# Two gated linear-attention branches: the low-weight terms of the last, half-filled chunk of K, Q and V moved into 64-row matmuls

## The chip, the cores and the metric

The kernel runs on one core of a Trainium2 chip, in float32 data (float32r operands for the large matmuls). The metric is the device time of one launch in microseconds (us); the smaller, the better. Engines are named as in the profile: PE (matmul), PEld (weight load into PE), DVE, ACT, POOL and SP (which issues the DMAs).

## The reference

Two branches A and B share x (2048 tokens, 448 features, 16 heads of 28) and are mixed by a gate:

```python
def branch(x, wqkv, w_phi, wo):                    # B=1, S=2048, D=448, H=16, Dh=28
    q, k, v = split_heads(x @ wqkv)
    pq, pk = q @ w_phi, k @ w_phi                  # per head, 28 x 28
    phi_q = concat(softmax(pq), softmax(-pq))      # 56 features
    phi_k = concat(softmax(pk), softmax(-pk))
    kv, z = phi_k.T @ v, phi_k.sum(over s)         # sums over all tokens
    return ((phi_q @ kv) / (phi_q @ z + 1e-6)) @ wo

g = sigmoid((x * gate_w).sum(-1))
out = g * branch(x, *A) + (1 - g) * branch(x, *B)
```

## The kernel before, in words

**Tiling.** The 2048 tokens are 16 tiles of 128. `xt`, the transposed x, and the weights come in chunks of 128 feature rows: 448 rows are three full chunks and one of 64 rows. The rows of the last chunk are there twice, so chunk 3 fills all 128 partitions. Every float32 operand is split into a high part (rounded to float32r) and a low part. For x, `split_x` (L306) makes chunks 0 to 3 of the high part, writes the low part of chunk 3 into the upper 64 partitions of chunk 3 itself, and puts the low parts of chunks 0 to 2 into chunks 4 to 6 (`xs`, seven chunks of 256 tokens for one pair of tiles, three such buffers).

**K, Q and V.** For a tile and a branch b, `mms` (L416) runs eleven matmuls into one PSUM bank, by the list `XT` (L414): (chunk of x, high or low weights, chunk of the weights).

```python
    XT = [(c, 0, c) for c in range(4)] + [(c, 1, c) for c in range(4)] + [(4 + c, 0, c) for c in range(3)]
```

Term (3, 0, 3) multiplies the high and the low half of x's last chunk with the high weights; term (3, 1, 3) multiplies both halves with the low weights, of which only the lower 64 partitions (high x times low weights) carry what is needed. `k_proj` (L471), `q_proj` (L511) and `v_proj` (L457) call `mms` for b = 0 and 1: banks `K0` and `K1`, the two banks of `Q`, and `VA` and `VB`. The projections for K and Q already contain `w_phi`, which `fold` put into the weights at the start.

**What follows a projection.** `v_out` (L463): ACT copies VA and VB into `vs`, and for branch A takes the gate's exponential into `glog`. `k_soft` (L475): ACT copies K0 and K1 into `pk`; then come two reductions on DVE, two subtractions on POOL, two exponentials on ACT, two sums on DVE and two multiplications on POOL, into one of three buffers `es`. `q_front` (L515): DVE reduces Q over the feature axis, subtracts, and SP sends the result through DRAM (`qd`) for a turn of the layout. `q_soft` (L532, steps "S") loads it back, makes both softmaxes (ACT, DVE, POOL) and transposes on DVE; for tiles 0 to 7 the result goes to DRAM (`spill`) until it is fetched back. `kv_acc` (L496, steps "kv") adds two tiles' states phi_k.T @ v into bank `T0` with small matmuls, `T<-ret,vs`, of 29 columns by 56.

**After the last tile.** The states are turned (`kv_turn`), and for every two tiles come 32 x 32 matmuls into four banks `N` (`num`, L581), a DVE transpose, a reciprocal, mixing by the gate on POOL, more transposes, and 21 matmuls per tile with the output weights into `O0` or `O1` (`out_mm`, L631).

**The order.** `steps` (L109) writes the order of the work out by hand. PE follows it strictly. On the other engines `Plan.order` (L53) sorts: each step has a cost and a due time worked out backwards along its dependencies, and a free engine takes the ready step that is due first. The instructions of an engine then run in that fixed order, each waiting for its inputs. In the loop over p in 2..6 of `steps` one iteration treats K of tiles 2p and 2p+1, Q of tiles 2p-2 and 2p-1, V of tiles 2p+2 and 2p+3, and one kv step in its middle, behind the first Q.

Of the kernel before, what the change touches and what calls it, by code (L numbers as in the profile page):

```python
# [13 lines left out]
P = 128  # L14
# [94 lines left out]
def steps():  # L109
# [4 lines left out]
    yield from (("S", 0, JIT % 3 - 1), ("K", 2), ("Q", 1), ("S", 1, (JIT - 1) % 3 - 1), ("k", 3, 0), ("k", 3, 1), ("vm", 5, 0), ("kv", 0, 1), ("vo", 5, 0), ("ks", 3), ("V", 5, 1))  # L114
    for p in range(2, 7):
        yield "x", p + 1
        yield "K", 2 * p
        yield "Q", 2 * p - 2
        if 2 * p - 2 < JIT:
            yield "S", 2 * p - 2, (JIT - 2 * p + 2) % 3 - 1  # L120
        yield "kv", 2 * p - 2, 2 * p - 1
        yield "wo", p - 2
        if p == 3:
            yield "wo", 6
        if p < 6:
            yield "V", 2 * p + 2
        yield "K", 2 * p + 1
        yield "Q", 2 * p - 1
        if 2 * p - 1 < JIT:
            yield "S", 2 * p - 1, (JIT - 2 * p + 1) % 3 - 1  # L130
        if p < 6:
            yield "V", 2 * p + 3
        if p == 6:
            yield "gates", 0, 12
            yield "gates_b", 0, 12
    yield from (("K", 14), ("V", 14, 0), ("k", 15, 0), ("k", 15, 1), ("kv", 12, 13), ("wo", 5), ("load_wo",), ("Q", 12), ("ks", 15), ("V", 14, 1), ("V", 15, 0), ("q", 13, 0), ("q", 13, 1))
# [30 lines left out]
def hedgehog_mix(ctx: ExitStack, tc: tile.TileContext, xd, wv, wkt, wqt, wphi, wo, cmask, cpmask, out):  # L167
# [18 lines left out]
    rq = sb.tile([P, 2, 8 * FW], F32R, name="rq")  # L186
    rx = sb.tile([P, NX, 14 * P], F32R, name="rx")
    ret = sb.tile([P, 3 * 2048 + NE * 4 * D], F32, name="ret")
# [50 lines left out]
    def free_v():  # L239
# [38 lines left out]
    def low_part(eng, n, o, a, h, r, w, **k):  # L278
        put(eng, n, tt(eng, o, a, h, OP.subtract), r, w, two=True, **k)
# [40 lines left out]

# [94 lines left out]

    def mms(t, w, name, k, lo, hi):  # L416
        x, o = xs[t // 2 % NX], t % 2 * P
        def go():
            for i, (xc, l, c) in enumerate(XT):
                nc.tensor.matmul(bank[name][:, k, lo:hi], x[:, xc, o:o + P], w[l][:, c], start=i == 0, stop=i == len(XT) - 1)  # L420
        return go

    def xkeys(t):
        return [("x", t // 2 % NX, t % 2), ("xl", t // 2 % NX, t % 2)]

    def feat(w, b):
        return [x[:, b].rearrange("p c f h -> p c (f h)") for x in w]
# [272 lines left out]
    for what, *a in steps():  # L700
# [125 lines left out]
```

## Time and profile before

| | us |
|---|---|
| median of 3 timed runs | 337.41 (337.08 to 338.82) |
| the profiled execution's own time | 338.86 |
| its span, first to last instruction of the program | 337.0 |
| PE busy / PEld busy | 329.7 / 295.5 |
| DVE busy / POOL busy / ACT busy | 280.6 / 250.8 / 145.2 |

The span is what the trace covers; the profiled execution's own time has 1.86 us more around it. A busy PE means that some matmul was in flight: matmuls overlap, each lasts 0.36 us in the record while a new one starts about every 0.2 us, so the busy share doesn't say how fast PE goes. What it costs is read from the distance between matmuls, and from the chain of work that ended last, which gives every piece the time by which it moved the end.

### The profile page before, as it was taken

What the parts mean: (1) busy time and instruction counts of PE and PEld (TensorE: products, weight loads), DVE (VectorE), ACT (ScalarE), POOL (GpSimd) and SP (SyncE); (2) the same over time, 40 slices, a digit from 0 to 9 for tenths busy, and PEclk for the clock granted to TensorE, in tenths of its full rate; (3) what the DMA queues carried; (4) which work ended last, traced back from release to release, by engine and by line L of the source; (5) the groups of instructions that cost most, each with busy time, mean ns of one, the idle gap of its engine ahead of it and who ended that gap; (6) DMA issues with size and microseconds to landing.
All of it is one profiled execution on the core that took longest, in us unless ns stands there. A gap on an engine that the chain in (4) does not pass through costs nothing.

```text
span 337.0 us, 8897 instructions
## 1 busy us (share of the span) xinstructions
PE 329.7 (98%) x3742; PEld 295.5 (88%) x3742; DVE 280.6 (83%) x339; ACT 145.2 (43%) x236; POOL 250.8 (74%) x210
## 2 busy tenths in 40 slices
PE   7999999999999999999999999999999999999994
PEld 6977899998999999999999999999788888788894
DVE  3648879699797896969899979797899999999960
ACT  3747944372365462624445344432052433523331
POOL 7018669999999969989896999694269768887400
PEclk9999999999999999999999999999999999999999
DMA  7773046531297757647646330765886355131011
GB/s 248 215 244 97 2 125 189 165 119 41 70 336 251 217 187 191 238 136 238 217 123 262 88 110 15 277 255 182 236 255 236 135 191 197 61 147 56 31 54 55
DMA packets 29871, 54.73 MB, mean 162 GB/s; under 512 B 4632, under 2 KB 25480, under 8 KB 27528
## 3 DMA queue, kind: packets, MB, share of 16 engines
q1 hardware_dynamic: 29576, 54.06, 48.7%
q8 instruction: 29, 0.48, 0.6%
q0 software_dynamic: 256, 0.12, 0.1%
q14 instruction: 10, 0.08, 0.1%
HBM read 31.54 MB, written 24.22 MB: 165 GB/s over the span
## 4 chain that ended last, share of the span: by engine, by line
PE 65%; DVE 18%; POOL 8%; DMA 4%; issue 3%; ACT 1%; SPq 1%; DVEq 0%; POOLq 0%; ACTq 0%
PE Q L420 15%; PE K L420 14%; PE O L636 10%; PE VA L420 8%; PE VB L420 8%; POOL ret L263 3%; PE T L505 3%; DVE rv L599 3%; POOL rv L608 3%; DVE ret L551 3%; PE N L588 2%; DMA ret<-in_wv 2%; DVE sm L493 2%; DVE rx L263 1%; DVE qsm L546 1%
## 5 line engine op out<-in xcount | busy, mean ns | idle before, releaser
L420 PE MATMUL Q<-rq,rx 128*128 128x432 f32 x352 | 72.1, 359 | 0.0
L420 PE MATMUL K<-rk,rx 128*128 128x432 f32 x352 | 71.8, 359 | 0.0
L636 PE MATMUL O<-rk,rx 128*128 128x448 f32 x336 | 70.6, 368 | 0.1
L636 PEld LDWEIGHTS O<-rk,rx 128*128 128x128 f32 x336 | 62.5, 188 | 8.5 <-ACT rx L627 1.2
L420 PEld LDWEIGHTS Q<-rq,rx 128*128 128x128 f32 x352 | 65.9, 188 | 3.8 <-DVE ru L263 0.4
L420 PEld LDWEIGHTS K<-rk,rx 128*128 128x128 f32 x352 | 66.1, 188 | 3.1
L266 ACT ACTIVATE ret<-ret 128x896 f32<-128x896 f32 x48 | 45.7, 951 | 46.3 <-POOL ret L263 45.3
L263 POOL TENSOR_TENSOR ret<-ret,sm 128x896 f32<-128x896 f32 x32 | 53.9, 1707 | 2.4 <-DVE sm L494 2.2
L493 DVE TENSOR_REDUCE sm<-ret 128x32 f32<-128x896 f32 x32 | 33.8, 1070 | 6.2 <-ACT ret L266 6.2
L551 DVE STREAM_TRANSPOSE ret<-ret 128x2048 f32<-128x2048 f32 x16 | 36.5, 2283 | 0.9 <-POOL ret L263 0.6
L263 POOL TENSOR_TENSOR ret<-pk,mx 128x896 f32<-128x896 f32 x16 | 27.3, 1707 | 11.6 <-DVE mx L486 11.6
L546 DVE TENSOR_REDUCE qsm<-ret 128x32 f32<-128x896 f32 x32 | 33.3, 1058 | 2.6 <-ACT ret L266 2.5
L420 PE MATMUL VA<-rv,rx 128*128 128x450 f32 x154 | 34.3, 370 | 0.0
L420 PE MATMUL VB<-rv,rx 128*128 128x448 f32 x154 | 33.9, 367 | 0.0
L263 POOL TENSOR_TENSOR ret<-qmn,ru 128x896 f32<-128x896 f32 x16 | 28.2, 1765 | 6.9 <-DVE ret L551 4.2
L266 ACT ACTIVATE ret<-ru 128x896 f32<-128x896 f32 x16 | 15.2, 951 | 42.1 <-issue 19.6
L420 PEld LDWEIGHTS VB<-rv,rx 128*128 128x128 f32 x154 | 28.6, 188 | 3.4 <-issue 0.8
L420 PEld LDWEIGHTS VA<-rv,rx 128*128 128x128 f32 x154 | 28.6, 189 | 2.9 <-ACT rk L266 0.4
L263 POOL TENSOR_TENSOR ret<-ret,qsm 128x896 f32<-128x896 f32 x16 | 27.3, 1705 | 0.9
L263 POOL TENSOR_TENSOR ret<-mx,pk 128x896 f32<-128x896 f32 x16 | 27.3, 1707 | 0.7 <-DVE mx L487 0.7
L540 DVE TENSOR_REDUCE qmn<-ru 128x32 f32<-128x896 f32 x16 | 17.0, 1062 | 10.6 <-DMA ru<-qd 10.5
L608 POOL TENSOR_TENSOR rv<-rv,rd 128x896 f32<-128x896 f32 x14 | 23.8, 1703 | 1.1
(92 smaller groups left out, 443.6 us busy)
## 6 DMA issues: line engine op xcount, KB each, us to landing
ed<-ret SPq DMA_DIRECT2D x8, 1024.0 KB
ret<-ed SPq DMA_DIRECT2D x8, 1024.0 KB
qd<-ru SPq DMA_DIRECT2D x64, 112.0 KB
ru<-qd SPq DMA_DIRECT2D x16, 448.0 KB
out<-ret SPq DMA_DIRECT2D x16, 224.0 KB
wod<-wst SPq DMA_DIRECT2D x14, 224.0 KB
rk<-wod SPq DMA_DIRECT2D x2, 1568.0 KB
xraw<-in_xt SPq DMA_DIRECT2D x5, 512.0 KB
```

The lines of the kernel that those rows point to most:

```text
L263: return lambda: ENG[eng].tensor_tensor(val(o), val(a), val(b), op)
L266: return lambda: A.activation(val(o), val(i), f, **k)
L420: nc.tensor.matmul(bank[name][:, k, lo:hi], x[:, xc, o:o + P], w[l][:, c], start=i == 0, stop=i == len(XT) - 1)
L493: put("DVE", 2 * D, lambda s=s, e3=e3: V.tensor_reduce(sm[:, s], e3, AX.X, OP.add), [ke[s], *([("u", 0, 1)] if t == 15 else [])], [("sm", ...
L505: nc.tensor.matmul(kvp()[32 * r:32 * r + DH + 1, b, g], vs[t % NV][:, b, h // 2, h % 2], es[t % NE][:, :, hs:hs + DH], start=(t == 0 and b ...
L540: put("DVE", 2 * D, lambda: V.tensor_reduce(qmn, tq.rearrange("p c b g f -> p c (b g) f"), AX.X, OP.min), [kt, *late], [kn])
L546: put("DVE", 2 * D, lambda s=s, e3=e3: V.tensor_reduce(qsm[:, s], e3, AX.X, OP.add), [ke[s], *late], [("qsm", i, s)])
L551: add("DVE", 2.25, lambda: V.transpose(eTf[slot], eq.rearrange("p s a c f -> p (s a c f)")), ke, turned(slot))
L588: nc.tensor.matmul(bank["N"][32 * g:32 * g + 32, r, 2 * b * P:2 * b * P + 2 * P], kvt[32 * r:32 * r + 32, b, s, g], eTp[slots[0] // 2][32 ...
L599: add("DVE", 0.07 + 1.08 * nt, lambda: V.transpose(ctr().rearrange("p (r n) -> p r n", r=4), bank["N"][:, :, :2 * nt * P]), ["N"], [("ctr" ...
L608: put(eng, 2 * D, lambda: ENG[eng].tensor_tensor(mid["o", n % 3].rearrange("p (c a f) -> p a c f", c=4, a=8), ctv()[:, :, i, :, :DH], rd[: ...
L636: nc.tensor.matmul(bank[pb][:, 0, :D], a, w, start=i == 0, stop=i == len(terms) - 1)
```

## The change

For the iterations p = 2 to 5 term (3, 1, 3) is left out of the eleven of K and Q (tiles 4 to 11 and 2 to 9) and of V (tiles 6 to 12): steps "k10", "q10" and "v10" run ten terms and leave the PSUM group open. A new step "halves" then closes the open groups of one K tile, one Q tile and (from V tile 6 on) one V tile at once, with two matmuls of 64 rows for each: branch 0 in partitions 0 to 63, branch 1 in partitions 64 to 127. For branch 1 the upper 64 partitions need the high part of x's last chunk, so `xs` gets an eighth chunk, which ACT fills from the upper copy of the raw rows (`xd`). The product of the low x with the low weights, which the full term added as well, is no longer in these tiles' sums.

Since a group stays open until "halves", all banks of K, Q and V close together; the copies and reductions that follow are listed behind "halves", V of the next tile runs right behind them, and V tiles 7, 9, 11, 13 and 15 use bank `O0` in place of `VA`. The kv step stands behind the second "halves" of an iteration rather than in its middle. Iteration p = 6 is written out with full terms. `wp` and `wpd`, which are needed only at the start, now lie in `kvt`, which is needed only at the end.

```diff
-    for p in range(2, 7):
+    for p in range(2, 6):
         yield "x", p + 1
-        yield "K", 2 * p
-        yield "Q", 2 * p - 2
-        if 2 * p - 2 < JIT:
-            yield "S", 2 * p - 2, (JIT - 2 * p + 2) % 3 - 1
-        yield "kv", 2 * p - 2, 2 * p - 1
-        yield "wo", p - 2
...
-        if p < 6:
-            yield "V", 2 * p + 2
-        yield "K", 2 * p + 1
-        yield "Q", 2 * p - 1
...
+        for i in range(2):
+            k, q, v = 2 * p + i, 2 * p - 2 + i, 2 * p + 1 + i
+            yield "k10", k
+            yield "q10", q
+            yield "halves", k, q, v if v >= 6 else None
+            if i:
+                yield "kv", q - 1, q
+            yield "ks", k
+            yield "qf", q
+            if v >= 6:
+                yield "vo", v, 0
+                yield "vo", v, 1
+            yield "S", q, (JIT - q) % 3 - 1
...
+            yield "v10" if k < 11 else "V", v + 1
+    yield from (("x", 7), ("K", 12), ("Q", 10), ("wo", 4), ("k", 13, 0), ("k", 13, 1), ("kv", 10, 11), ("ks", 13), ("Q", 11), ("gates", 0, 12), ("gates_b", 0, 12))
...
-    rx = sb.tile([P, NX, 14 * P], F32R, name="rx")
+    rx = sb.tile([P, NX, 16 * P], F32R, name="rx")
...
-    wp = sb.tile([P, 2, 4, HP], F32, name="wp")
-    wpd = sb.tile([P, 2, 4, HP], F32, name="wpd")
...
+    wp, wpd = kvt[:, 0], kvt[:, 1]
...
+        if p < 7:
+            put("ACT", hi - lo, act(t[64:P, 7, :], r[64:P, 3, :]), [*kr, *l], [("xd", n, i) for i in range(lo // P, hi // P)])
...
-    def mms(t, w, name, k, lo, hi):
+    def mms(t, w, name, k, lo, hi, part=False):
         x, o = xs[t // 2 % NX], t % 2 * P
+        terms = [a for a in XT if not part or a != (3, 1, 3)]
         def go():
-            for i, (xc, l, c) in enumerate(XT):
-                nc.tensor.matmul(bank[name][:, k, lo:hi], x[:, xc, o:o + P], w[l][:, c], start=i == 0, stop=i == len(XT) - 1)
+            for i, (xc, l, c) in enumerate(terms):
+                nc.tensor.matmul(bank[name][:, k, lo:hi], x[:, xc, o:o + P], w[l][:, c], start=i == 0, stop=i == len(terms) - 1 and not part)
         return go
+
+    def halves(k, q, v):
+
+        keys, banks_, go = [], [], []
+        for t, kind in ((v, "v"), (k, "k"), (q, "q")):
+            if t is not None:
+                x, o = xs[t // 2 % NX], t % 2 * P
...
+                    banks_.append(kb)
+                    go.append((name, i, lo, n, x[64 * b:64 * b + 64, 7 if b else 3, o:o + P], w[64 * b:64 * b + 64, 3]))
+        def run():
+            for name, i, lo, n, a, w in go:
+                nc.tensor.matmul(bank[name][:, i, lo:lo + n], a, w, start=False, stop=True)
+        add("PE", 0.3 + 0.1 * len(go), run, keys, list(dict.fromkeys(banks_)))
...
     def v_bank(t, b):
-        return (f"K{b}", 0, ("K", b)) if t == 1 else (("VA", "VB")[b], 0, ("VA", "VB")[b])
+        n = "O0" if b == 0 and t >= 7 and t % 2 else ("VA", "VB")[b]
+        return (f"K{b}", 0, ("K", b)) if t == 1 else (n, 0, n)
```

The first place is PE in the iteration p = 3. K_99, K_100 (K_97, K_98 in the changed kernel) are the banks K0 and K1, O_556 is O0, T_557 is T0. Before:

```order
L420 MATMUL K_99<-rk,rx 128x432 x11
L420 MATMUL K_100<-rk,rx 128x432 x11
L420 MATMUL Q<-rq,rx 128x432 x22
L505 MATMUL T_557<-ret,vs_74 29x56 x32
L505 MATMUL T_557<-ret,vs_70 29x56 x32
L420 MATMUL VA<-rv,rx 128x450 x11
L420 MATMUL VB<-rv,rx 128x448 x11
```

and in the changed kernel, the second half of iteration p = 3:

```order
L422 MATMUL VA<-rv,rx 128x450 x10
L422 MATMUL VB<-rv,rx 128x448 x10
L422 MATMUL K_97<-rk,rx 128x432 x10
L422 MATMUL K_98<-rk,rx 128x432 x10
L422 MATMUL Q<-rq,rx 128x432 x20
L447 MATMUL VA<-rv,rx 128x450
L447 MATMUL VB<-rv,rx 128x448
L447 MATMUL K_97<-rk,rx 128x432
L447 MATMUL K_98<-rk,rx 128x432
L447 MATMUL Q<-rq,rx 128x432 x2
L533 MATMUL T_557<-ret,vs_74 29x56 x32
L533 MATMUL T_557<-ret,vs_70 29x56 x32
```

Each of the six banks has one full matmul less, and six matmuls of 64 rows (L447) stand in a row behind the last full one; the kv step follows them.

The second place is ACT where it empties the banks of V tile 7 and K tile 6; in the changed kernel these close in one "halves", and VB must be empty before V of tile 8 may use it, K0 before K of tile 7. Before:

```order
L266 ACTIVATE ret<-ru 128x32x28
L266 ACTIVATE vs_72<-VB 128x16x28
L266 ACTIVATE wst<-wst 128x448
L266 ACTIVATE ret<-ret 128x32x28
L266 ACTIVATE pk_68<-K_99 128x448
L266 ACTIVATE pk_68<-K_100 128x448
```

and in the changed kernel:

```order
L265 ACTIVATE ret<-ret 128x896 x2
L265 ACTIVATE ret<-ru 128x32x28
L265 ACTIVATE vs_72<-VB 128x16x28
L265 ACTIVATE pk_68<-K_97 128x448
L265 ACTIVATE pk_68<-K_98 128x448
L265 ACTIVATE vs_72<-O_556 128x16x28
L265 ACTIVATE glog<-O_556 128x1
```

The copies out of PSUM now stand side by side, and VB's stands behind exponentials that wait for POOL (`ret<-ret`) and for a DMA (`ret<-ru`).

## Rows read from the trace of the kernel before

**Rows 1.** The page: busy time, and the granted clock in 40 slices of the span.

```profile
PE 329.7 (98%) x3742; PEld 295.5 (88%) x3742; DVE 280.6 (83%) x339; ACT 145.2 (43%) x236; POOL 250.8 (74%) x210
PEclk9999999999999999999999999999999999999999
```

**Rows 2.** Waits of PE: engine, line, who was waited for; total us, times, longest.

```profile
PE VA L452 <- ACT rv L266: 1.1, 1, 1.1
PE VB L645 <- DVE zero L654: 1.1, 1, 1.1
PE T L505 <- POOL ret L263: 0.7, 1, 0.7
```

**Rows 3.** The chain that ended last, 98 to 139 us: start us, us, what.

```profile
98.52 4.32 PE K L420 x22
102.84 4.31 PE Q L420 x22
107.14 1.71 PE T L505 x128
108.85 2.45 PE VA L420 x11
111.31 2.23 PE VB L420 x11
...
122.16 2.26 PE VA L420 x11
...
136.99 2.44 PE VA L420 x11
```

**Rows 4.** The same chain from 231 us on.

```profile
236.48 2.70 PE N L588 x115
239.21 2.33 DVE rv L599
...
292.48 3.52 PE O L636 x16
```

**Rows 5.** Timeline of PE at the kv step of 78 us: start us, us, what.

```profile
78.05 0.99 PE L505 MATMUL T<-ret,vs 128*29 128x56 f32 x64
79.74 0.99 PE L505 MATMUL T<-ret,vs 128*29 128x56 f32 x64 [0.70 <-POOL ret L263]
80.67 0.87 PE L420 MATMUL VA<-rv,rx 128*128 128x450 f32 x3
```

**Rows 6.** Timeline of PE where it changes from full to small matmuls and back.

```profile
106.78 0.36 PE L420 MATMUL Q<-rq,rx 128*128 128x432 f32 x1
107.07 1.78 PE L505 MATMUL T<-ret,vs 128*29 128x56 f32 x128
...
108.78 0.47 PE L420 MATMUL VA<-rv,rx 128*128 128x450 f32 x1
```

**Rows 7.** Timeline of PE and PEld behind a group of N; N's durations (ns, min/median/max).

```profile
257.54 0.46 PE L588 MATMUL N<-ret,kvt 32*32 32x256 f32 x6
257.92 0.48 PE L636 MATMUL O<-rk,rx 128*128 128x448 f32 x1
...
257.92 0.30 PEld L636 LDWEIGHTS O<-rk,rx 128*128 128x128 f32 x2 [0.41 <-issue]
...
L588 PE MATMUL N<-ret,kvt x1024: 373/375/400, 236.4 to 315.1; 32*32 32x256 f32 x171
```

**Rows 8.** Groups of matmuls and loads: count, busy us, mean ns of one.

```profile
L420 PE MATMUL VA<-rv,rx 128*128 128x450 f32 x154 | 34.3, 370 | 0.0
...
L420 PEld LDWEIGHTS K<-rk,rx 128*128 128x128 f32 x352 | 66.1, 188 | 3.1
...
L588 PEld LDWEIGHTS N<-ret,kvt 32*32 32x32 f32 x1024 | 14.4, 103 | 6.2 <-issue 1.8 <-DVE qsm L546 0.3 <-DVE rv L625 0.3
```

**Rows 9.** Three iterations: PE, PEld, DVE, ACT, POOL busy; clock; DMA share; GB/s.

```profile
79.64:107.77 28.13, 28.03 (x252) 26.29 (x256) 23.66 (x28) 12.81 (x21) 27.54 (x22) 1.00 0.59 200
107.77:135.90 28.13, 28.13 (x276) 26.39 (x268) 22.90 (x27) 13.50 (x21) 25.11 (x18) 1.00 0.65 204
135.90:164.02 28.12, 28.12 (x277) 26.36 (x268) 24.23 (x30) 13.04 (x21) 24.86 (x18) 1.00 0.64 217
```

**Rows 10.** ACT: copies out of VB and K, its copies of x, and its waits.

```profile
113.57 0.55 ACT L266 ACTIVATE vs<-VB 128x448 f32<-128x448 f32 x1 [1.62 <-PE VB L420]
...
115.74 0.54 ACT L266 ACTIVATE pk<-K 128x448 f32<-128x448 f32 x1 [0.33 <-PE K L420]
...
L266 ACT ACTIVATE rx<-xraw x8: 402/1042/1062, 4.5 to 180.8; 128x1024 fp32r<-128x1024 f32 x5, 128x512 fp32r<-128x512 f32 x2, 128x256 fp32r<-128x256 f32 x1
...
ACT ret L266 <- POOL ret L263: 45.3, 35, 6.5
```

**Rows 11.** Windows ahead of the last phase and in it, columns as in rows 9.

```profile
220.00:240.00 20.00, 20.00 (x334) 17.67 (x333) 16.70 (x26) 4.07 (x9) 11.14 (x8) 1.00 0.67 228
260.00:280.00 20.00, 20.00 (x305) 16.97 (x304) 19.55 (x21) 7.42 (x12) 14.93 (x15) 1.00 0.50 178
```

More of the change, by code (lines that the diff above doesn't have):

```diff
@@ L114, in steps @@
     yield from (("S", 0, JIT % 3 - 1), ("K", 2), ("Q", 1), ("S", 1, (JIT - 1) % 3 - 1), ("k", 3, 0), ("k", 3, 1), ("vm", 5, 0), ("kv", 0, 1), ("vo", 5, 0), ("ks", 3), ("V", 5, 1))
[L115 removed]
+    for p in range(2, 6):
         yield "x", p + 1
[L117 to L135 removed]
+        for i in range(2):
[11 more added lines that the diff above has]
+            yield "S", q, (JIT - q) % 3 - 1
+            if i == 0:
+                yield "wo", p - 2
+                if p == 3:
+                    yield "wo", 6
+            yield "v10" if k < 11 else "V", v + 1
+    yield from (("x", 7), ("K", 12), ("Q", 10), ("wo", 4), ("k", 13, 0), ("k", 13, 1), ("kv", 10, 11), ("ks", 13), ("Q", 11), ("gates", 0, 12), ("gates_b", 0, 12))
     yield from (("K", 14), ("V", 14, 0), ("k", 15, 0), ("k", 15, 1), ("kv", 12, 13), ("wo", 5), ("load_wo",), ("Q", 12), ("ks", 15), ("V", 14, 1), ("V", 15, 0), ("q", 13, 0), ("q", 13, 1))
@@ L221, in hedgehog_mix @@
     wvh, wvl = (rv[:, i].rearrange("p (c n) -> p c n", c=4) for i in range(2))
-    xs = [rx[:, i].rearrange("p (k t) -> p k t", k=7) for i in range(NX)]
+    xs = [rx[:, i].rearrange("p (k t) -> p k t", k=8) for i in range(NX)]
     es = [re[:, i].rearrange("p (s n) -> p s n", s=2) for i in range(NE)]
@@ L245, in free_v @@
         mid["oT", 0], mid["oT", 1] = f[:, 6784:7168], ref[:, 4992:5376]
-    hls = [rx[:, i].rearrange("p (s k t) -> p s k t", s=2, k=7) for i in range(NX)]
+    hls = [rx[:, i, :14 * P].rearrange("p (s k t) -> p s k t", s=2, k=7) for i in range(NX)]
     obs = [ref[:, 4096 + D * i:4096 + D * i + D] for i in range(2)]
@@ L414, in hedgehog_mix @@
     XT = [(c, 0, c) for c in range(4)] + [(c, 1, c) for c in range(4)] + [(4 + c, 0, c) for c in range(3)]
-    def mms(t, w, name, k, lo, hi):
+    def mms(t, w, name, k, lo, hi, part=False):
         x, o = xs[t // 2 % NX], t % 2 * P
+        terms = [a for a in XT if not part or a != (3, 1, 3)]
         def go():
-            for i, (xc, l, c) in enumerate(XT):
-                nc.tensor.matmul(bank[name][:, k, lo:hi], x[:, xc, o:o + P], w[l][:, c], start=i == 0, stop=i == len(XT) - 1)
-        return go
+            for i, (xc, l, c) in enumerate(terms):
+                nc.tensor.matmul(bank[name][:, k, lo:hi], x[:, xc, o:o + P], w[l][:, c], start=i == 0, stop=i == len(terms) - 1 and not part)
+        return go
+    def halves(k, q, v):
[3 more added lines that the diff above has]
+                x, o = xs[t // 2 % NX], t % 2 * P
+                keys += xkeys(t) + [("xd", t // 2 % NX, t % 2)]
+                for b in range(2):
+                    if kind == "v":
+                        (_, w), n = v_weights(b)
+                        name, i, kb = v_bank(t, b)
+                        lo = 0
+                        keys.append(("vl", 3, b))
+                    else:
+                        w = feat(((wkh, wkl), (wqh, wql))[kind == "q"], b)[1]
+                        name, i, kb = (f"K{b}", 0, ("K", b)) if kind == "k" else ("Q", b, "Q")
+                        lo, n = FO, FZ - FO
+                        keys += wkeys(kind, (b,))
+                    banks_.append(kb)
[4 more added lines that the diff above has]
+        add("PE", 0.3 + 0.1 * len(go), run, keys, list(dict.fromkeys(banks_)))
     def xkeys(t):
@@ L455, in v_first, with v_proj @@
             v_out(t, b)
-    def v_proj(t, b):
+    def v_proj(t, b, part=False):
         w, n = v_weights(b)
         n_, k, kb = v_bank(t, b)
-        add("PE", 11 * 0.203, mms(t, w, n_, k, 0, n),
+        add("PE", (11 - part) * 0.203, mms(t, w, n_, k, 0, n, part),
             xkeys(t) + [("v" + h, c, b) for h in "hl" for c in range(4)], [kb])
@@ L469, in v_out, with k_proj @@
             add("ACT", 0.2, act(glog[:, t:t + 1], lambda: bank[n_][:, k, D:D + 1], AF.Exp, scale=-1.0), [kb], [("gl", t)], ahead=9.0 * (t < 2))
-    def k_proj(t, b):
-        add("PE", 11 * 0.197, mms(t, feat((wkh, wkl), b), f"K{b}", 0, FO, FZ),
+    def k_proj(t, b, part=False):
+        add("PE", (11 - part) * 0.197, mms(t, feat((wkh, wkl), b), f"K{b}", 0, FO, FZ, part),
             xkeys(t) + wkeys("k", (b,)), [("K", b)])
@@ L509, in kv_acc, with q_proj @@
             [k for t in ts for k in (("e", t % NE, 0), ("e", t % NE, 1), ("v", t % NV, 0), ("v", t % NV, 1))], ["T0"])
-    def q_proj(t, b):
-        add("PE", 11 * 0.197, mms(t, feat((wqh, wql), b), "Q", b, FO, FZ),
+    def q_proj(t, b, part=False):
+        add("PE", (11 - part) * 0.197, mms(t, feat((wqh, wql), b), "Q", b, FO, FZ, part),
             xkeys(t) + wkeys("q", (b,)), ["Q"])
@@ L720, in hedgehog_mix @@
             q_front(*a)
+        elif what in ("k10", "q10", "v10"):
+            for b in range(2):
+                {"k": k_proj, "q": q_proj, "v": v_proj}[what[0]](*a, b, True)
+        elif what == "halves":
+            halves(*a)
         elif what == "Q":
```

## The prediction

> **What bounds the kernel now.** I read the page first. PE is busy for 98% of the span and its granted clock reads 9 tenths or more in every slice [rows 1], 1.00 in the middle [rows 9], the upper of its two levels (2.4 GHz), so no slow clock explains the time. But DVE is at 83% and POOL at 74%, so the page alone doesn't settle the bound. PE's waits do: three in all, two of them at the start and one of 0.7 us behind POOL [rows 2]. The chain that ended last then shows from 98 us on nothing but PE, piece behind piece: 22 matmuls of K in 4.32 us, 22 of Q in 4.31, eleven of V in 2.23 or 2.26 [rows 3]. One matmul of 432 columns thus costs 4.32/22 = 0.196 us, one of 448 or 450 about 2.245/11 = 0.204. The distance follows the columns, though a weight load alone lasts 0.188 us in the record [rows 8]. From 239 us on the chain runs over DVE, until it comes back to PE at 292 [rows 4]. So in the stretch that the change touches (about 67 to 180 us) PE is the bound, and a matmul taken out is worth its distance, if nothing else becomes late.
>
> **Terms taken out and put in.** K loses one term in 8 tiles and 2 branches, Q as many: 32 x 0.196 = 6.27 us. V loses it in 7 tiles: 14 x 0.204 = 2.86. Together 9.13 us. In their place come 46 matmuls of 64 rows, in 23 pairs whose two members use different halves of the rows and different banks. No matmul of 64 rows is in this trace. From below a pair costs one slot (0.196 or 0.204), from above two. The nearest rows are those of N, 32 x 32 pieces of 256 columns, whose group has 115 of its matmuls in 2.70 us, 0.023 each [rows 4]. By the distance above, 256 columns one after another would take 256/432 x 0.196 = 0.116 us each; so about five run at a time. I take one slot: 23 pairs cost 16 x 0.196 + 7 x 0.204 = 4.56, and **4.57 us** are saved.
>
> **Changes of shape.** PE goes from full rows to half rows and on in eight places. What such a change costs is in the trace. The last Q starts at 106.78 and the first T at 107.07 [rows 6]: 0.29 in place of 0.196, so 0.095 for letting the array run empty. The first V behind T then lasts 0.47 us, where its kind has a mean of 0.370 [rows 6, 8]: 0.10 for a weight load that nothing covers. The way in costs about 0.095 + 0.10 = 0.20 us, as the half-row load has 128 columns like the full one. For the way out I have two neighbours: behind Q the emptying costs the same 0.095; behind N the last matmul starts at 257.54 + 0.46 - 0.375 = 257.625 and the first O at 257.92, 0.295 in place of 0.116, so 0.18 [rows 7]. Half rows lie between the two shapes, so I take 0.14. In four of the eight places full rows follow (0.14 + 0.10 = 0.24); in the other four T follows, which paid 0.095 for its way in before and now pays 0.14, so 0.045 more, and T's way out is as before. Sum: 8 x 0.20 + 4 x 0.24 + 4 x 0.045 = **2.7 us lost**. The terms net 4.57 - 2.74 = 1.8 us. A middle iteration (two trips of three pairs) should shrink by 0.5, from 28.1 to 27.6 us; the first has one trip of two pairs and shrinks by 0.3.
>
> The Trainium skill says, in TensorEngine Tiling (Array Packing), Key Properties, that a change of tiling mode, not merely of tile, drains TensorE; its Overview promises up to twice the speed for 64 rows. By the second alone the terms would give 4.6 us, with the first 1.8; the trace agrees with the first, by the 0.095 and 0.18 us above.
>
> **The kv step.** At 78 us T's first 64 matmuls start at 78.05, the other 64 wait for POOL until 79.74, and V follows at 80.67 [rows 5]. That is 2.62 us, against 107.07 to 108.78 = 1.71 in the next iteration [rows 6]. In the changed kernel this step stands half an iteration (some 13 us) later, while the multiplications it waits for ended at 79.7. So **0.9 us** go. What would be late next is the split of x for V of tile 6, which PE now reaches at 78; its subtractions on POOL stand ahead of K's there, and no step of K needs POOL sooner than the kv step does. I take nothing for it.
>
> **Edits at nothing.** ACT gets eight copies of 64 partitions: four of 256 columns, at most 0.40 us each by the 256-column form, and four of 128 [rows 10]; under 3 us in all on an engine at 43% [rows 1]. If that cover fails, a copy holds up what stands behind it on ACT (a rival below). `wp` in `kvt`, the larger `rx` and V in `O0` use space that is idle then. POOL's and DVE's work is only reordered; POOL has 27.5, 25.1 and 24.9 us in iterations of 28.1 [rows 9], so it fits into 27.6, barely in the first. SP issues the same DMAs, though the load of x and those of the output weights change places with q's; q's load is needed a whole half-iteration later.
>
> **Does the end follow?** The chain's DVE part begins with the transpose at 239.21, which N's end releases [rows 4], and in the 20 us before, DVE works 16.7 and POOL 11.1 us [rows 11]; neither carries a backlog there, so what PE gains ahead of N arrives at the end.
>
> **Sum.** 1.8 + 0.9 = 2.7 us. The profiled execution goes from 338.86 to 336.2 and its span from 337.0 to 334.3. The median of the timed runs is 1.45 below that execution, so I forecast **334.7** for it. With a drain of 0.095 or 0.18 on every way out and some tenths for small waits, this case reaches from 333.9 to 335.6. About 0.5% (1.7 us, so 335.7 and 339.1) is what a measurement of this kernel can tell from no change.
>
> **The rivals.**
> Loads in series: the two loads of a pair go one after the other. Two full loads behind N start 0.30 - 0.19 = 0.11 us apart [rows 7]; a pair then takes 0.22 in place of 0.198 (23 x 0.022 = 0.5 lost), and each way in shows a second bare load (8 x 0.11 = 0.9). The gain falls to 1.3: 336.1. For it: a load of 32 columns lasts 103 ns and a full one 188 [rows 8], so columns count. Against: N's loads come as often as its matmuls, every 0.023 us. The Trainium skill, TensorE: Matmul & The Clock Gate, LDWEIGHTS, speaks for the first step of this rival: the time of a load follows its columns alone, so half the rows save nothing. 15%.
> No overlap: pairs need two slots. Then only the changes of shape and the kv step remain: 337.4 + 2.74 - 0.9 = **339.3, slower**. It decides where a pair takes over 0.198 + 2.7/23 = 0.32 us, and by over 0.5% near two slots. For it: T's 56 columns would take 0.025 us each alone and take 1.71/128 = 0.013, so only two of its four column pieces overlap. Against: N. 8%.
> ACT is late: VB is read behind "halves" and written again behind ten terms, 0.24 + 2.05 us later, of which the copy takes 0.55 [rows 10]; 1.7 us are left in the three places without T. ACT runs in order, and its exponentials waited for POOL 35 times, at most 6.5 us [rows 10]. If such a wait reaches 1.7 us past "halves", PE stands: 1 us in all of three places gives 337.7, 2 us 340.7. Before, K, Q and VA lay between, 4.32 + 4.31 + 2.26 us [rows 3]. 12%.
> The end doesn't follow: DVE has 19.6 of 20 us in the last phase [rows 11]. If its backlog, not N, set the start, the gain would be lost: 337.4. 8%.
> Cheaper changes: half rows need no drain, and the change does all its terms promise: 337.4 - 4.57 - 0.9 = 331.9. 7%.
>
> **How the numbers follow.** My forecast has 50%. Faster by over 0.5%: 50 + 7, a quarter of loads in series (4) and 2 of the late ACT, 0.63. Slower by over 0.5%: most of no overlap (6) and 5 of the late ACT, 0.11. Within: 0.26. The range takes the forecast, loads in series, the lost end and a late ACT of up to 1 us: 332.6 to 338.0; outside lie the other cases and half of the cheap one.
>
> **What would show it.** Right: in the timeline a first half-row matmul 0.29 us behind the last Q, pairs 0.2 apart, and the next shape 0.3 behind the last pair; V to V in the chain 27.6 us; no wait of T; no wait of PE for ACT. Wrong: pairs 0.3 or more apart, "PE VB <- ACT" or "PE K <- ACT" among the waits, or a last phase that starts earlier and ends no earlier.

## The result, and the profile of the changed kernel

| | before | changed |
|---|---|---|
| median of 20 timed executions | 337.78 us | 339.73 us |
| their range | 336.96 to 340.93 | 336.59 to 341.82 |
| profiled execution: own time, span | 338.86, 337.0 | 340.17, 338.4 |

The ratio is 1.0046, 95% interval [1.0025, 1.0067]: the changed kernel is half a per cent slower, where 0.8% faster was forecast. (Ratios leave out executions that lie over 1.5% above the fastest of their kernel.)

The page's busy times, PE's waits, and three iterations from one end of Q to the next but one (columns as in rows 9):

```profile
PE 329.1 (97%) x3742; PEld 290.4 (86%) x3742; DVE 284.5 (84%) x339; ACT 146.8 (43%) x244; POOL 251.0 (74%) x210
PEclk9999999999999999999999999999999999999999
```
```profile
PE Q L422 <- DVE ru L262: 3.1, 1, 3.1
PE VB L673 <- DVE zero L682: 1.1, 1, 1.1
PE VA L480 <- ACT rv L265: 0.5, 1, 0.5
PE K L422 <- ACT pk L265: 0.3, 1, 0.3
PE Q L422 <- ACT rk L265: 0.3, 1, 0.3
```
```profile
79.06:106.68 27.62, 27.62 (x262) 24.99 (x261) 23.93 (x28) 12.13 (x20) 27.23 (x21) 1.00 0.54 187
106.68:134.31 27.63, 27.63 (x262) 25.02 (x261) 25.14 (x28) 12.70 (x22) 25.28 (x19) 1.00 0.63 212
134.31:161.93 27.62, 27.62 (x262) 25.01 (x261) 24.12 (x29) 13.76 (x23) 25.58 (x19) 1.00 0.64 213
```

The iterations did shrink, from 28.13 [rows 9] to 27.62 us, and PE has no gap in them; T's wait [rows 2] is gone. But PE now stands 3.1 us in front of a Q, which it never did before. Two stretches of PE's timeline show the gain and the loss, half rows first (start us, us, what):

```profile
117.71 0.76 PE L422 MATMUL Q<-rq,rx 128*128 128x432 f32 x3
118.40 0.47 PE L447 MATMUL VA<-rv,rx 64*128 64x450 f32 x1
118.40 0.47 PE L447 MATMUL VB<-rv,rx 64*128 64x448 f32 x1
118.70 0.37 PE L447 MATMUL K<-rk,rx 64*128 64x432 f32 x2
118.89 0.37 PE L447 MATMUL Q<-rq,rx 64*128 64x432 f32 x2
119.20 0.40 PE L533 MATMUL T<-ret,vs 128*29 128x56 f32 x16
...
188.61 0.94 PE L422 MATMUL Q<-rq,rx 128*128 128x432 f32 x4
189.85 0.65 PE L422 MATMUL K<-rk,rx 128*128 128x432 f32 x2 [0.30 <-ACT pk L265]
...
195.60 0.53 PE L533 MATMUL T<-ret,vs 128*29 128x56 f32 x28
199.23 0.66 PE L422 MATMUL Q<-rq,rx 128*128 128x432 f32 x2 [3.10 <-DVE ru L262]
```

The two members of a pair start together (their weight loads at 118.39 and 118.40, 0.18 us each); pairs are 0.30 and 0.19 us apart, and T follows 0.31 behind the last. The Q that ends at 189.55 is tile 10's, the one at 199.23 tile 11's. It waits for the bank that DVE empties with `qmx` (the maximum) and two subtractions into `ru`. DVE's timeline there, of the changed kernel and then of the kernel before:

```profile
187.74 1.09 DVE L521 TENSOR_REDUCE sm<-ret 128x32 f32<-128x896 f32 x1 [2.72 <-ACT ret L265]
...
191.74 1.07 DVE L574 TENSOR_REDUCE qsm<-ret 128x32 f32<-128x896 f32 x1
192.72 1.08 DVE L514 TENSOR_REDUCE mx<-pk 128x32 f32<-128x896 f32 x1
193.72 1.08 DVE L515 TENSOR_REDUCE mx<-pk 128x32 f32<-128x896 f32 x1
194.71 2.30 DVE L579 STREAM_TRANSPOSE ret<-ret 128x2048 f32<-128x2048 f32 x1
196.94 1.05 DVE L548 TENSOR_REDUCE qmx<-Q 128x32 f32<-128x896 f32 x1
198.02 1.16 DVE L262 TENSOR_TENSOR ru<-Q,qmx 128x448 f32<-128x448 f32 x2
```
```profile
185.41 1.07 DVE L493 TENSOR_REDUCE sm<-ret 128x32 f32<-128x896 f32 x1
...
188.33 1.03 DVE L486 TENSOR_REDUCE mx<-pk 128x32 f32<-128x896 f32 x1
189.27 1.07 DVE L487 TENSOR_REDUCE mx<-pk 128x32 f32<-128x896 f32 x1
...
191.25 1.07 DVE L546 TENSOR_REDUCE qsm<-ret 128x32 f32<-128x896 f32 x1
192.24 1.08 DVE L520 TENSOR_REDUCE qmx<-Q 128x32 f32<-128x896 f32 x1
193.36 1.15 DVE L263 TENSOR_TENSOR ru<-Q,qmx 128x448 f32<-128x448 f32 x2
...
198.94 2.25 DVE L551 STREAM_TRANSPOSE ret<-ret 128x2048 f32<-128x2048 f32 x1
```

`qmx` of tile 10 now starts 7.4 us behind the end of Q and not 0.7, and PE had only K of tile 13 and a kv step (6.0 us) to do in between. Before, the transpose of state 8 came behind `qmx` of tile 10 (at 198.94; eight transposes of states stand ahead of that `qmx` in the whole trace). Now it is the ninth and stands ahead of it, 2.2 us. The two reductions of K of tile 12 (`mx<-pk`) stand ahead of it in both kernels, but before they were done at 188 to 190 us, while Q of tile 10 still ran. And DVE is late already at the sum for K of tile 11 (`sm<-ret`, at 187.74), where it stands 2.7 us for ACT's exponential. That one waits for a subtraction on POOL, which comes at 185.00 and not at 181.70; POOL's timeline, changed kernel first:

```profile
179.25 0.23 POOL L597 TENSOR_SCALAR gate<-gate 128x48 f32<-128x48 f32 x1 [1.43 <-DMA gate<-gd]
...
182.39 2.67 POOL L262 TENSOR_TENSOR rx<-xraw,rx 64x256 fp32r<-64x256 f32 x2
185.00 1.72 POOL L262 TENSOR_TENSOR ret<-pk,mx 128x896 f32<-128x896 f32 x1
```
```profile
181.70 1.70 POOL L263 TENSOR_TENSOR ret<-pk,mx 128x896 f32<-128x896 f32 x1
```

A stand for the gates' data and the split of x (`rx<-xraw,rx`) now come ahead of it. In the chain that ended last, the stretch from 100 to 199 us is no longer PE, as in [rows 3], but the way of q through DVE, DRAM, DVE, POOL and ACT.

The start-up differs by up to 2.1 us between the traces of the runs below. To compare spans, I count from DVE's first `qmx` (tile 0), behind the start-up: 51.20 before and 51.88 in the changed kernel. From there to the end it is 337.0 - 51.20 = 285.8 us before and 286.5 now. By the same mark PE ends Q of tile 10 after 137.7 us, before after 140.3: the 2.7 us that the sum forecast are there. `qmx` of tile 10, however, starts after 145.1 us, before after 141.0: 4.0 us later, of which 2.2 are the transpose and 1.7 the late sum (187.74 and 185.41, each from its mark). The wait of 3.1 us and 0.3 ahead of K of tile 13 take more than the 2.7, and the end comes 0.7 later. The medians lie 2.0 apart; what makes up the rest is not shown by these two traces.

### The profile page after: what moved, and what is told of

It is laid out like the page before. It is cut to its first block, busy times and chain, and to the rows that moved or that the text cites. A ratio compares the mean times of both kernels' runs of the same rounds, so it can differ in the third digit from the quotient of the medians.

```text
span 338.4 us, 8908 instructions
## 1 busy us (share of the span) xinstructions
PE 329.1 (97%) x3742; PEld 290.4 (86%) x3742; DVE 284.5 (84%) x339; ACT 146.8 (43%) x244; POOL 251.0 (74%) x210
## 4 chain that ended last, share of the span: by engine, by line
PE 40%; DVE 23%; POOL 13%; DMA 12%; ACT 4%; issue 4%; SPq 2%; DVEq 0%; POOLq 0%; ACTq 0%
PE O L664 10%; PE K L422 9%; PE Q L422 9%; POOL ret L262 7%; DVE ret L579 6%; DMA qd<-ru 5%; DMA ru<-qd 4%; POOL rv L636 3%; PE VA L422 3%; PE VB L422 3%; DVE rv L627 3%; DVE ru L262 2%; SPq L268 2%; DVE qmx L548 2%; DVE qsm L574 2%
## 5 line engine op out<-in xcount | busy, mean ns | idle before, releaser
L422 PE MATMUL Q<-rq,rx 128*128 128x432 f32 x336 | 69.3, 360 | 3.4 <-DVE ru L262 3.1
L422 PEld LDWEIGHTS Q<-rq,rx 128*128 128x128 f32 x336 | 62.8, 188 | 7.3 <-DVE ru L262 3.7
L422 PE MATMUL K<-rk,rx 128*128 128x432 f32 x336 | 68.7, 359 | 0.3 <-ACT pk L265 0.3
L422 PEld LDWEIGHTS K<-rk,rx 128*128 128x128 f32 x336 | 63.0, 188 | 3.6 <-ACT pk L265 0.7
L422 PE MATMUL VB<-rv,rx 128*128 128x448 f32 x147 | 32.5, 368 | 0.0
L422 PEld LDWEIGHTS VB<-rv,rx 128*128 128x128 f32 x147 | 27.2, 188 | 3.5 <-issue 0.8
L616 PE MATMUL N<-ret,kvt 32*32 32x256 f32 x1024 | 22.1, 385 | 0.0
L422 PE MATMUL VA<-rv,rx 128*128 128x450 f32 x95 | 21.4, 372 | 0.0
L265 ACT ACTIVATE pk<-K 128x448 f32<-128x448 f32 x32 | 16.3, 539 | 11.1 <-PE K L422 8.1
```

Of the source, the lines that this page charges most:

```text
L265: return lambda: A.activation(val(o), val(i), f, **k)
L616: nc.tensor.matmul(bank["N"][32 * g:32 * g + 32, r, 2 * b * P:2 * b * P + 2 * P], kvt[32 * r:32 * r + 32, b, s, g], eTp[slots[0] // 2][32 ...
```

## The experiments

Theory A: the matmuls save what the sum said, and a new wait, made by the order on DVE, takes it. Rival B: DVE, POOL and q's round trip set the pace anyway, so no order helps. Rival C: half rows cost more than counted. The edits are to the changed kernel; each run's medians stand beside those of the kernel before on the same chip. A ratio is the run to the kernel before, with its 95% interval; one that holds 1 shows no difference.

**Q of tile 10 first on DVE** (what empties its bank goes ahead of the reductions of K of tile 12; state 9's transpose, named in the edit, stood behind it anyway):

```
-            yield "S", q, (JIT - q) % 3 - 1
+            if q < 9:
+                yield "S", q, (JIT - q) % 3 - 1
...
-    ("x", 7), ("K", 12), ("Q", 10), ("wo", 4), ...
+    ("x", 7), ("k", 12, 0), ("k", 12, 1), ("Q", 10), ("ks", 12), ("S", 9, 0), ("wo", 4), ...
-        kp = [(*kp, b) for b in range(2)]
+        kp = [(*kp, b) for b in range(2)] + ([("u", 0, 0), ("u", 0, 1)] if t == 12 else [])
-        add("DVE", 2.25, lambda: V.transpose(eTf[slot], ...), ke, turned(slot))
+        add("DVE", 2.25, lambda: V.transpose(eTf[slot], ...), ke + ([("u", 0, 0), ("u", 0, 1)] if k == 9 else []), turned(slot))
```

> In the changed kernel PE reaches the end of Q of tile 10 some 2.0 us sooner than before (2.7 if the later start of PE is set aside), and then Q of tile 11 waits 3.1 us for the reduction that empties the Q bank. DVE had done the reductions of K of tile 12 and the transpose of state 9 ahead of that reduction, in the order the planner fixed. This kernel keeps the change whole and puts the reduction of Q of tile 10 (and what follows from it) ahead of those. Theory A (a new wait, made by the order on DVE, takes the gain): PE's wait of 3.1 us at Q of tile 11 shrinks to under 0.5, and the time falls by 2 to 3 us, to 335.5 to 337.5, a ratio to the kernel before of about 0.995. Rival B (the loop over DVE, POOL and the round trip of q through DRAM is itself the bound from 100 us on, so that no order helps): the wait moves to another place within two tiles, the time stays at 339 to 340.5, a ratio of 1.003 to 1.006. Rival C (half rows cost more than counted): no change either, and no wait of PE in place of this one; the time lies in the distances of its matmuls.

Measured: 338.36 us (before 337.83), ratio 1.0009 [0.9984, 1.0033]. The wait shrinks by 2.0 us, but not to nothing, and a new gap opens ahead of the first N. PE's waits, and DVE's timeline at `qmx` of tile 10:

```profile
PE Q L423 <- DVE ru L263: 1.1, 1, 1.1
PE N L617 <- issue: 1.1, 1, 1.1
...
PE VB L423 <- ACT vs L266: 0.7, 2, 0.4
```
```profile
193.23 2.30 DVE L580 STREAM_TRANSPOSE ret<-ret 128x2048 f32<-128x2048 f32 x1
195.46 1.05 DVE L549 TENSOR_REDUCE qmx<-Q 128x32 f32<-128x896 f32 x1
```

The reductions of K are out of the way, the transpose of state 8 is not; no run moves it.

N shows no releaser, but it starts (237.79) when DVE ends `kvt`, the transposes of the summed state, which stand behind a minimum (`qmn`) whose data comes late from DRAM:

```profile
235.87 1.08 DVE L569 TENSOR_REDUCE qmn<-ru 128x32 f32<-128x896 f32 x1 [2.44 <-DMA ru<-qd]
236.88 0.76 DVE L604 STREAM_TRANSPOSE kvt<-kvs 128x256 f32<-128x256 f32 x2
237.56 0.28 DVE L606 TENSOR_SCALAR kvt<-kvt 128x4 f32<-128x4 f32 x2
```

So A holds for two thirds of the first wait, and B's "it moves" for part of it. The time lies between the two forecasts (337.5 at most by A, 339 at least by B), and its interval holds 1.

**Full rows for the half rows** (the order of every engine unchanged):

```
-    go.append((name, i, lo, n, x[64 * b:64 * b + 64, 7 if b else 3, o:o + P], w[64 * b:64 * b + 64, 3]))
+    go.append((name, i, lo, n, x[:, 3, o:o + P], w[:, 3]))
```

> The order of every engine is that of the changed kernel; only the 46 matmuls of 64 rows now run with all 128 rows (both branches one after the other), so the sums also take products of rows that the 64-row form leaves out, and for K, Q and V of the tiles in question the result differs in the low part. Without changes of shape PE loses 23 x 0.197 = 4.5 us for the second member of each pair and gains back 2.7 us of shape changes: some 1.8 us later at the end of Q of tile 10. Theory A: PE arrives 1.8 us later at a bank that is emptied at the same time, so the wait of 3.1 us shrinks to about 1.3 and the time stays within 0.5 us of the changed kernel (ratio to before 1.003 to 1.006). Rival B says the same of the time. Rival C (halves cost more than full rows): PE is sooner at Q of tile 10 and the time falls below 338.5. If PE were still the bound, the time would rise by 1.8, to 341.5.

Measured: 339.26, ratio 1.0044 [1.0024, 1.0065], as the changed kernel. From the end of Q of tile 1 to that of tile 9 PE takes 117.15 us in place of 115.02, so half rows save 2.1 us there; the wait falls from 3.1 to 1.6. Rival C is out, and so is PE as the bound.

**The operation on the gates later on POOL:**

```
     def gates_b(lo, hi, after=()):
...
-            [("ga", lo, r) for r in range(4)] + list(after), [("gate", t) ...
+            [("ga", lo, r) for r in range(4)] + list(after) + ([("e", 0, 1)] if lo == 0 else []), [("gate", t) ...
```

> In the changed kernel POOL stands 1.43 us at 178 us, behind an operation on the gates whose data comes back from DRAM at 179.06; what stands behind it on POOL reaches ACT and DVE late, and the reduction of Q of tile 10 with them. Here that operation alone is put some 17 POOL operations later. Theory A with this cause: POOL's gap at 178 goes, the reduction of Q of tile 10 and so Q of tile 11 come 0.7 to 1.4 us sooner, and the time falls by as much, to 338.3 to 339 (ratio 1.000 to 1.003). If the order on DVE alone makes the lateness, the gap goes and the wait of 3.1 us stays within 0.4, with the time as that of the changed kernel. Rival B: the gap goes and the wait moves by up to 1.4, but the end stays.

Measured: 339.02, ratio 1.0031 [1.0008, 1.0054]; the wait falls to 2.4, and by the mark `qmx` of tile 10 starts after 143.9 us, 1.2 sooner than in the changed kernel: most of the 1.7 us of the late sum hung on this operation. The time is at the upper end of what was expected.

**V of tile 14 into the gap:**

```
-    ... ("ks", 13), ("Q", 11), ...
-    yield from (("K", 14), ("V", 14, 0), ("k", 15, 0), ...
+    ... ("ks", 13), ("V", 14, 0), ("Q", 11), ...
+    yield from (("K", 14), ("k", 15, 0), ...
```

> Between the end of Q of tile 10 and the start of Q of tile 11 the changed kernel gives PE only K of tile 13 and the kv step (6.0 us). Here the first half of V of tile 14 (eleven matmuls, 2.2 us), which needs no bank that is late, stands there too and is missing later. Nothing is saved on PE; the Q bank only has 2.2 us more to be emptied in. Theory A: the wait of 3.1 us shrinks to about 0.9 and the time falls by up to 2.2 us, to 337 to 338.5 (ratio 0.996 to 1.002). Rival B: the wait shrinks, but PE waits as much further on (Q of tiles 12 or 13), and the time stays at 339 to 340.5. Rival C: no statement.

Measured: 338.79, ratio 1.0030 [1.0007, 1.0053]; two waits of 0.7 and 0.6 at Q (tiles 11 and 13) remain, and 0.4 ahead of N. The time lies between A's forecast (338.5 at most) and B's (339 at least).

**The transposes of the summed state first**, alone and with the others:

```
-    ... AX.X, OP.min), [kt, *late], [kn])
+    ... AX.X, OP.min), [kt, *late] + ([("kvt", 0), ("kvt", 1)] if k == 12 else []), [kn])
```

> In two of the experiments that shortened the wait at Q of tile 11, PE then stood 0.5 to 1.1 us ahead of the first N (at 237): N needs the transposes of the summed state (kvt), and DVE does these behind the minimum of q of tile 12, whose data comes back from DRAM only at 235.8. This kernel is the changed kernel with those transposes put ahead of that minimum on DVE, and nothing else. Theory A2 (two waits, one behind the other: the Q bank at tile 11 takes the gain, and the place at N would take part of it if the first were gone): alone this edit gives nothing, because in the changed kernel PE comes to N 0.3 us behind kvt; 339 to 340, ratio 1.003 to 1.006, the wait of 3.1 us unchanged. Rival D (the start of N is what sets the end whatever PE does before): the first N starts 0.5 to 1 us sooner and the time falls by as much, to 338.7 to 339.2.

Measured: median 340.85 (before 338.29), ratio 1.0015 [0.9979, 1.0051] from six of the twelve executions; PE's wait still 3.1 us. No gain is shown, as A with two waits (A2) said, but the interval is too wide to tell A2's time from D's. The traces speak against D: in the changed kernel `kvt` is done at 237.32, 0.8 us ahead of the first N (238.12), which starts right behind the last Q; so N did not wait for `kvt`, and here too it starts behind the last Q.

> Both edits: the reduction of Q of tile 10 first on DVE, and the transposes of the summed state ahead of the minimum of q of tile 12. Theory A2: the 1.1 us ahead of N that the first edit alone left go as well; PE's waits are then 1.1 at Q of tile 11 and some tenths behind ACT; the time falls by about 1.1 from that of the first edit alone (338.36), to 336.8 to 337.6, ratio 0.996 to 0.999. Rival B (DVE and POOL are the bound, every wait only moves): N starts no sooner, or what is gained is lost in the last phase; 338.4, ratio 1.001.

Measured: 337.17, ratio 0.9985 [0.9958, 1.0012]. The gap ahead of N is gone (0.29 us, a change of shape). The median is where A2 put it; the interval holds 1.

> The first half of V of tile 14 ahead of Q of tile 11, and the transposes of the summed state ahead of the minimum of q of tile 12. Theory A2: the 0.5 us ahead of N go, the waits of 0.8 us at Q of tile 11 and 0.7 us at Q of tile 13 stay; 0.5 less than with V of tile 14 alone (338.79): 338.0 to 338.5, ratio 1.000 to 1.003. Rival B: 338.8, ratio 1.003.

Measured: 338.75 (before 338.29), ratio 1.0010 [0.9990, 1.0030]. The median is that of V of tile 14 alone, as B said; the ratio is 0.2% lower, as A2 said; the intervals overlap, so this run does not decide. The gap ahead of N went, but this execution waits 0.9 at a VB behind ACT.

> All three edits: the reduction of Q of tile 10 first, the first half of V of tile 14 ahead of Q of tile 11, and the transposes of the summed state ahead of the minimum of q of tile 12. Theory A2: no wait of PE at Q of tile 11 and none ahead of N; what is left is some tenths behind ACT and up to 1 us at Q of tile 13, whose bank DVE empties late, as it did when V of tile 14 was moved alone. The time is 335.5 to 337, ratio 0.993 to 0.998: faster than before by most of the 2.7 us that the sum of the prediction gave. Rival B: PE's waits sum to 2 us or more wherever they lie, and the time is 338 to 339, ratio 1.000 to 1.003.

Measured: 337.37, ratio 0.9976 [0.9953, 1.0000], between A2's forecast (337 at most) and B's (338 at least); PE waits 0.8 at Q of tile 13 and 0.7 at a VB.

**No half rows at all:**

```
-            for name, i, lo, n, a, w in go:
-                nc.tensor.matmul(bank[name][:, i, lo:lo + n], a, w, start=False, stop=True)
+            pass
```

The last full term of each group closes it instead.

> The changed kernel without its 46 matmuls of 64 rows: their products (the last 64 rows of the split, both branches, of K and Q in eight tiles and of V in seven) are left out of the result; the order of every engine is unchanged, and the copies on ACT stay. PE has 23 x 0.198 + 2.7 = 7.3 us less to do ahead of Q of tile 10. If PE were the bound in the half iterations and only the order at tile 10 took the gain (theory A2), the emptying of the Q bank would come sooner as well, by most of 7.3, and the time would fall to 333 to 336. Rival B (from 100 us on the loop of DVE, POOL and the round trip of q through DRAM sets the pace, at some 13.2 us for a half iteration where PE needs 13.8, or 12.7 without the half rows): the emptying of the Q bank of tile 10 comes at most 2 us sooner, PE waits 5 us or more at Q of tile 11 or in the half iterations, and the time is 337 to 341.

Measured: 339.57 (five executions), ratio 1.0066 [1.0041, 1.0092]: with 7.3 us of PE's work left out, by the prediction's terms, not faster. PE's waits and DVE's timeline:

```profile
PE VB L422 <- ACT vs L265: 3.4, 3, 2.9
PE Q L422 <- DVE ru L262: 3.1, 1, 3.1
```
```profile
51.19 1.07 DVE L547 TENSOR_REDUCE qmx<-Q 128x32 f32<-128x896 f32 x1
...
196.30 1.06 DVE L547 TENSOR_REDUCE qmx<-Q 128x32 f32<-128x896 f32 x1
```

From `qmx` of tile 0 to that of tile 10 DVE takes 145.11 us; in the changed kernel 196.94 - 51.88 = 145.06. With full rows, where PE needs 2.1 us more, it is 145.10. What PE saves up to there does not move DVE. Here B is right: between tile 0 and tile 10 the order on DVE, with its waits for q's data and POOL, sets when the bank comes free, and PE's saving becomes a wait. But its "no order helps" is wrong: with the order of the kernel before it is 141.0 us.

**A filled gap.** In 16 of the changed kernel's 20 timed executions the mean granted clock was 0.993 to 0.995; in the kernel before it was 0.997 or more in 104 of the 105 that were timed beside the experiments. The windows of the experiment with the gates show where it goes, at the Q behind the wait (columns as in rows 9):

```profile
196.00:198.00 2.00, 0.78 (x4) 0.76 (x5) 2.00 (x3) 1.73 (x4) 0.72 (x1) 1.00 0.00 0
198.00:200.00 2.00, 2.00 (x8) 1.81 (x7) 2.00 (x3) 0.13 (x1) 0.00 (x0) 0.51 0.86 213
200.00:202.00 2.00, 2.00 (x8) 1.86 (x7) 2.00 (x5) 0.00 (x0) 1.72 (x2) 0.64 0.16 32
```

In this run eleven matmuls of V of tile 14 go into VA in the gap, and are overwritten later:

```
-    ... ("ks", 13), ("Q", 11), ...
+    ... ("ks", 13), ("fill", 14), ("Q", 11), ...
```

> In the timed executions of the changed kernel the mean granted clock is 0.993 to 0.995 in 16 of 20 and 0.999 or 1.000 in four, where the kernel before has 0.997 or more in all. In the trace of an experiment with the same wait of 3.1 us at Q of tile 11, nine matmuls behind that wait stand 0.36 us apart in place of 0.196, at a granted clock of 0.50. Theory E (the wait has a second cost: behind it the clock often falls to its lower level for about 3 us, some 1.5 us lost): here PE repeats eleven matmuls of V of tile 14 (2.25 us, overwritten later) in the gap ahead of Q of tile 11, which changes no other engine's order and no bank that is late; the start of Q of tile 11 stays, 3.3 us behind T, but the wait that is left is 0.9 us. By theory E the mean clock is then 0.997 or more in most executions and the time falls by about 1.2, to 338.2 to 338.8. Without it the time stays at 339.5 to 340.

Measured: 341.64, ratio 1.0105 [1.0069, 1.0140] from six executions. The clock stayed at 1.000 in four of the six, as theory E said, but these took 339.1 to 342.8 us. In the profiled one, the fastest, PE stands 0.6 us within the second N with no releaser. Theory E's time is not met, and why the others are slower still is open. Among the changed kernel's own executions the four with a clock of 0.999 or 1.000 took 336.6, 339.8, 340.2 and 340.4 us, no less at the median than the sixteen others; with the gates later the four with 0.995 or less took 339.7 to 340.2, the eight others 338.4 at the median. How much of the changed kernel's median the clock accounts for is not shown.

**All four edits** (Q of tile 10 first, V of tile 14 into the gap, the summed state first, the gates later):

> The three edits of the last experiment (Q of tile 10 reduced first, the first half of V of tile 14 ahead of Q of tile 11, the transposes of the summed state first) and the operation on the gates later on POOL. With the three alone PE still waited 0.8 at Q of tile 13, 0.7 at V of tile 12 behind ACT and some tenths at K of tile 13. Theory A2: POOL's gap of 1.4 us at 178 goes, the reductions on DVE from tile 10 on come up to 1 us sooner, and PE's waits after 100 us shrink to under 0.8 in all; 336.0 to 337.2, ratio 0.993 to 0.998. Rival B: no better than the three, 337.4 or more.

Measured: 335.65 (before 337.98), ratio **0.9938 [0.9913, 0.9963]** from six executions. PE's waits are all in the start-up but one:

```profile
PE VB L673 <- DVE zero L682: 1.1, 1, 1.1
PE VA L480 <- ACT rv L265: 0.6, 1, 0.6
PE VB L422 <- ACT vs L265: 0.2, 1, 0.2
```
```profile
188.78 1.07 DVE L574 TENSOR_REDUCE qsm<-ret 128x32 f32<-128x896 f32 x1
189.76 2.30 DVE L579 STREAM_TRANSPOSE ret<-ret 128x2048 f32<-128x2048 f32 x1
191.99 1.05 DVE L548 TENSOR_REDUCE qmx<-Q 128x32 f32<-128x896 f32 x1
```

The span from `qmx` of tile 0 (50.60) to its end (333.8) is 283.2 us, 2.6 less than before, and `qmx` of tile 10 starts 141.4 us behind that mark, 3.7 sooner than in the changed kernel, though the transpose of state 8 still stands ahead of it. This version beats both kernels.

**The same edits on the kernel before** (those three that apply to it):

> The kernel before with the three of the four edits that apply to it (it has Q of tile 10 ahead on DVE already): the first half of V of tile 14 ahead of Q of tile 11, the transposes of the summed state first on DVE, the operation on the gates later on POOL. Whose gain is the 0.6% of all four edits? If it belongs to the change, and the edits only bring its 2.7 us to the end (theory A2), then here, where PE has no such waits, they give nothing: 337.5 to 338.3, ratio 0.998 to 1.002. If the edits are worth as much by themselves, the time falls to 335.5 to 336.5, ratio about 0.994.

Measured: 337.72 (before 338.41), ratio 0.9991 [0.9974, 1.0009]. The gain of the four edits is the change's. In this trace the kv step at 78 us, whose code is untouched, took 2.00 us, only 0.3 above the 1.71 of the next one, and not the 0.9 of [rows 5].

**Full rows with all four edits:**

> All four edits on the changed kernel, and its 46 matmuls of 64 rows run with all 128 rows, one branch after the other (the result then also holds the products of rows that the 64-row form leaves out); every engine's order is that of the kernel with all four edits. There PE waits for nothing between 100 and 290 us, so that its work should count in full: the half rows save 4.5 us of terms and pay 2.7 for changes of shape, 1.8 in all. Theory A2: 1.2 to 1.8 us more than with all four edits (335.65), 336.9 to 337.5, ratio 0.997 to 0.999; some tenths less than 1.8, since PE waits 0.3 for ACT without it. If the half rows save nothing net: 335.4 to 335.9, ratio 0.994.

Measured: 336.92 (before 338.41), ratio 0.9969 [0.9942, 0.9995]. The median is 1.27 us above that with all four edits, the ratio 0.3% (1.05 us), and from the mark to the end the traces give 284.75 to 283.2, 1.55. That is most of what PE saves by half rows, where it waits for little; but the two ratios' intervals overlap, so the size is not settled.

## Why the prediction was wrong

- **Terms and changes of shape: right.** Net 1.8 us were predicted, 2.1 measured on PE with waits aside (full rows against half rows), and 1.05 to 1.55 at the end where hardly a wait hides them. The first half row came 0.29 us behind the last Q, as said; pairs were 0.19 apart behind the first, which shows its bare load (0.30). T came 0.31 behind the last pair, where the sum took 0.34. "Loads in series" and "no overlap" fell: the members of a pair start 3 to 17 ns apart. The Trainium skill, TensorEngine Tiling (Array Packing), says in Key Properties that a change of mode drains TensorE: these rows agree, at 0.09 to 0.11 us for a drain. The Trainium skill's rule on loads (TensorE: Matmul & The Clock Gate, LDWEIGHTS), which spoke for loads in series, does not decide here, since the two loads of a pair overlap.
- **The kv step: right on PE, its size from one execution.** T's wait of 0.7 us is gone. The 0.9 came from a single profile; another one of the same step shows 0.3.
- **"Edits at nothing" failed.** The sentence was "POOL's and DVE's work is only reordered", and it was weighed by their busy time against the iteration's length. The iterations did hold it: PE has no gap in them. But a reorder on an engine that runs in a fixed order has its price at the one buffer whose release moves back, and that was the Q bank at tile 10, where the loop of half iterations ends and the hand-written tail begins. Its `qmx` came 4.0 us later and PE 2.7 sooner, and PE stood 3.1 us. 2.2 of the 4.0 are state 8's transpose, newly ahead of that `qmx` in DVE's order, which was to be had before the run; 1.7 came with POOL's order, where a stand for the gates' data and the split of x got ahead of K's subtractions; moving the gates took 1.2 of it back, the share of the split is argued only. The experiments show that the wait hangs on when this `qmx` comes: with the reductions of K out of its way 2.0 us of the wait went, with the gates later 0.7. What the transpose alone costs was not tried. The prediction weighed only the half iterations.
- **"Does the end follow?" failed too.** It asked whether DVE had a backlog in the 20 us ahead of N. The gain was lost 40 us earlier, and at a second place (`kvt` behind a late `qmn`) only 0.8 us were left in the changed kernel, so that it showed once the first wait was shortened.
- **The rivals.** "ACT is late" had the right kind (PE stands, 1 to 2 us in each of three places, 337.7 to 340.7) and the wrong engine: in the kernels with half rows ACT costs 0.2 to 0.9 us at VB or K, DVE 3.1. That its range holds the 339.7 is luck. Its 12% was the only weight on a new wait. With a chain that is PE alone over many us, I took slack of the other engines for granted; DVE at 83% had little.

## What to carry to other kernels

When an engine is the bound by a few per cent only, price a saving on it by when its buffers come free: list, for every buffer it writes, what stands ahead of the emptying instruction in its engine's order, before and after, and what those instructions wait for in turn. Here the order broke at the seam between a loop and a tail. When a gain does not arrive, take the first wait away and look for the next one: here three were stacked (Q of tile 11, Q of tile 13, N), and only with all of them gone did 2.3 of the 2.7 us show.

## What was not expected of the hardware

- Behind a wait of 2.4 us of PE (the gates later) Q started at 197.22 at a granted clock of 1.00, which then fell to 0.51 from 198 to 200 us (the lower of its two levels, 1.2 GHz), was 0.64 on average up to 202 and 1.00 from there on. The 22 matmuls of that Q took 6.15 us, in the changed kernel's profile 4.58. Executions with a mean clock of 0.995 or less: 16 of 20 and 9 of 12 in the two kernels with half rows and a wait of 3.1 us in the profile, 5 of 5 in the run without half rows (3.1 and 2.9), 4 of 12 with 2.4, 1 of 12 with 1.6, none of 6 with 0.2; but also 2 of 6 with the filled gap, whose longest wait behind the start-up is 0.6. In the changed kernel's own profile the clock stayed at 1.00 behind the 3.1 us, so it is not certain in any one execution.
- Two 64-row matmuls in different halves of the rows take one slot, with their loads: a pair of 432 columns follows the next 0.19 us later, as one full matmul does.
